# Attention into a max-out FFN: weight products ahead of batch 0, a log-and-exp softmax for batch 0, softmax steps issued singly

## The chip, the cores and the metric

The kernel runs on one core of a Trainium2 chip. The metric is the time of one execution on the device in microseconds (us), the median of several executions.

The engines have short names in the profile: PE multiplies matrices (PEld is its loading of weights), DVE works on vectors, ACT evaluates functions and copies, POOL and SP here mainly start transfers (DMAs). Each engine works through its own queue in order.

## The reference, cut to what matters

For each of 8 batches and 8 heads, a sequence of 576 positions is first summed into 32 memory slots, and then each position reads from those slots. The result, 4608 rows of 512, goes through an FFN with the maximum of three products as its activation.

```python
# q, k, v: (8, 8, 576, 64)   phi: (8, 8, 576, 32)   w1, w2, w3: (512, 768)   w_out: (768, 512)
a = np.exp(phi - max over positions);  a = a / (sum over positions)
k_m = einsum('bhsm,bhsd->bhmd', a, k)
v_m = einsum('bhsm,bhsd->bhmd', a, v)
scores = (q @ k_m.T) / 8
attn = softmax(scores over the 32 slots)
x = attn @ v_m                       # heads side by side: 4608 x 512
h = np.maximum(np.maximum(x @ w1, x @ w2), x @ w3)
out = h @ w_out
```

## The kernel before, in words

**Algebra.** Three rearrangements carry the kernel. First, max(x w1, x w2, x w3) is written as max(x (w1-w3), x (w2-w3), 0) + x w3. Hence `w_diff` subtracts w3 from w1 and w2 in place, a relu takes the place of one maximum, and the x w3 part goes straight to the output through w3 @ w_out, which is computed once (`w3_t` transposes w3, `w3_o` multiplies by w_out). Second, x is never formed: x w = attn (v_m w), so per batch `fold` multiplies the small v_m (32 slots per head) by w1-w3, w2-w3 (giving `wp`) and by w3 @ w_out (giving `wp3`). Third, phi has no maximum taken out before its exp; the normalisation is a division of the sums by the sum of exps, which a column of ones beside k and v delivers.

**Steps of one batch.** The letters are those of the order at the end of the kernel:

- L, H: load phi, k, v, q (0, 1, 2, 3); H loads half of batch 0's k or v. phi of batch 0 goes through SP's queue, every other load through POOL's, which also converts to bf16. Y: load w1, w2, w3 (0, 1, 2) or w_out (3), also on POOL.
- E: `att_exp`, exp of phi on ACT. B: `att_kv`, the sums over positions of k, v and ones on PE (72 small matmuls); part 0 is k and ones, part 1 is v alone. N: `att_kv_norm`, on DVE, divides the sums. K: `att_kv_t` transposes them on PE and copies the result out as `kvt`. Q: `att_q`, two 32x32-block transposes of q on DVE.
- S: `att_score`, scores on PE in two groups of heads (g = 0, 1), each with its exp on ACT to `e2`.
- X: `att_mul`, the softmax over slots for one group, five DVE instructions in a row: block transpose to `t` (line 313), sum (315), reciprocal (316), multiplication (317), transposing back into `attn` (323).
- D: `fold`, copied out by ACT or DVE. F: `ffn1`, 12 groups per batch, each of 4 matmuls of 288 columns (line 367); an even one ends in a relu (to `h1`), an odd one in a maximum with it on DVE (line 380, to `hT`). T: `ffn2`, a tile of 128 output rows, 8 matmuls of 512 columns (lines 398, 407), a copy and a store through SP. T4 is the tile that straddles two batches.
- W: `w3_t`. O: `w3_o`. V: `w_diff`. I: the identity. Z: n warm-up matmuls on a tile of zeros (line 128), whose result nobody reads.

**Buffers.** All PSUM tiles share one pool, `acc_pool`, of four tiles; a matmul group waits until an earlier tile has been read. `work` holds two of each tile. `evacuate` chooses between ACT and DVE by a table, and "!" behind a step swaps its choice:

```python
    EVAC = {"D": "avaaa", "T": "vavav", "K": "v", "W": "vvv", "O": "aaaa", "F": "aaaaaa"}
```

**Order.** The schedule is written out by hand: a string of steps such as `F8@0` (step F, number 8, batch 0), issued one after the other. This fixes each engine's queue; semaphores alone decide when a queued instruction starts. The first lines before:

```
        H3@0 H0@0 H2@0 I@0 H1@0 E@0 Z38@0 B@0 L3@0 N@0 Y2@0 Z3@0 K@0 Q0@0 Q1@0 Z7@0 S@0 X0@0
        Z6@0 W2@0! W0@0 Y3@0 Y0@0 W1@0 Z10@0 O1@0 O3@0 X1@0 V1@0 V0@0 O2@0 O0@0 D1@0 Y1@0 L0@1
```

So POOL loads v, k, q of batch 0, then w3, w_out, w1, w2, then batch 1; PE does batch 0's sums and scores first, then the w3 products, then the folds of batch 0 by the already subtracted weights.

Of the kernel before, what the change touches and what calls it, by code (L numbers as in the profile page):

```python
# [15 lines left out]
def kernel(  # L16
# [24 lines left out]
    FT = DF // P
    SH = S // 2
# [76 lines left out]
    warm = const.tile([P, BANK], BF16, name="warm")  # L119
    nc.vector.memset(warm, 0.0)  # L120
    nc.vector.memset(kvos[0][:, 2], 1.0)
    nc.vector.memset(kvos[1][:, 2], 1.0)

    def warm_up(n):
# [44 lines left out]

    w12 = w_sb[:, :, 0:2].rearrange("p j i f -> p j (i f)")  # L170

    FIRST = {0: (0, 512), 1: (512, 768), 2: (768, 1024), 4: (1024, 1536)}

    def columns(b, n):
        return FIRST[n] if b == 0 else (n * BANK, (n + 1) * BANK)

    def w_diff(n):

        c, end = FIRST[n]
        while c < end:  # L180
            e = min(end, (c // DF + 1) * DF)
            nc.vector.tensor_tensor(
                out=w12[:, :, c:e],
                in0=w12[:, :, c:e],
                in1=w_sb[:, :, 2, c % DF : c % DF + e - c],
                op=ALU.subtract,
            )
            c = e

    st = {}

# [56 lines left out]
    def att_kv_t(b, swap, part=None):  # L251

        s = st[b]
        ns = {None: slice(0, 3), 0: slice(1, 3), 1: slice(0, 1)}[part]
        ps = acc_pool.tile([P, 3, P], BF16, name="kvtp", tag="acc")
        for n in range(3)[ns]:
            nc.tensor.transpose(ps[:, n], s["kvn"][:, n], ident)
        if part != 1:
            s["kvt"] = work.tile([P, 3, P], BF16, name="kvt")
        evacuate("K", 0, swap, s["kvt"][:, ns], ps[:, ns])  # L260

    def att_q(b, n):

# [12 lines left out]
    def att_score(b):  # L276

        s = st[b]
        kvt, qT = s["kvt"], s["qT"]
        e2 = s["e2"] = work.tile([P, NG, S], BF16, name="e2")  # L280
        if b % 2 == 0:
            attns[b // 2] = work.tile([P, NG, 2 * S], BF16, name="attn")
        sc = [
            acc_pool.tile([P, 2, BANK], FP32, name="sc", tag="acc") for _ in range(NG)
        ]
        for h in range(2):
            for j in range(NP):
                for a in range(NG):
                    for t in range(2):
                        r = slice(R * (2 * a + t), R * (2 * a + t + 1))  # L290
                        nc.tensor.matmul(  # L291
                            sc[a][M * j : M * (j + 1), t, 0:SH],
                            lhsT=kvt[r, 1 + h, M * j : M * (j + 1)],
                            rhs=qT[r, j, :, :, h],
                            start=(h == 0),
                            stop=(h == 1),
                            tile_position=(R * (2 * a + t), M * j),
                        )
        for a in range(NG):
            nc.scalar.activation(  # L300
                out=e2[:, a].rearrange("p (t r c) -> p t r c", t=2, c=NC),
                in_=sc[a][:, :, 0:SH].rearrange("p t (c r) -> p t r c", c=NC),
                func=AF.Exp,
                scale=0.125,
            )

    def att_mul(b, g):
        s = st[b]
        e2 = s["e2"][:, g]
        t = work.tile([P, S // HP, R, 2], BF16, name="t", tag=f"t{g}")  # L310
        tf = t.rearrange("p n r e -> p (n r e)").bitcast(FP32)
        tv = t.rearrange("p n r e -> p n e r")
        nc.vector.transpose(out=tf, in_=e2.bitcast(FP32))  # L313
        sm = work.tile([P, S // HP, 2], FP32, name="sm", tag=f"sm{g}")
        nc.vector.tensor_reduce(out=sm, in_=tv, op=ALU.add, axis=mybir.AxisListType.X)  # L315
        nc.vector.reciprocal(out=sm, in_=sm)  # L316
        nc.vector.tensor_tensor(  # L317
            out=t,
            in0=t,
            in1=sm.unsqueeze(2).to_broadcast([P, S // HP, R, 2]),  # L320
            op=ALU.mult,
        )
        nc.vector.transpose(  # L323
            out=attns[b // 2][:, g, (b % 2) * S : (b % 2 + 1) * S].bitcast(FP32), in_=tf
        )

    wps, wp3s = {}, {}
# [1 line left out]
    def fold(b, n, swap):  # L329

        s = st[b]
        lo, hi = (0, DM) if n == 3 else columns(b, n)
        if n == 3:
            wp3s[b] = quad.tile([P, NG, DM], BF16, name="wp3")
        elif b not in wps:
            wps[b] = work.tile([P, NG, 2 * DF], BF16, name="wp")
        ps = acc_pool.tile([P, NG, BANK], FP32, name="wps", tag="acc")
        for j in range(NP):
            for a in range(NG):
                r = slice(HP * a, HP * (a + 1))  # L340
                nc.tensor.matmul(  # L341
                    ps[M * j : M * (j + 1), a, 0 : hi - lo],
                    lhsT=s["kvt"][r, 0, M * j : M * (j + 1)],
                    rhs=(w3o if n == 3 else w12)[r, j, lo:hi],
                    start=True,
                    stop=True,
                    tile_position=(HP * a, M * j),
                )
        evacuate(
            "D", n, swap, wp3s[b] if n == 3 else wps[b][:, :, lo:hi], ps[:, :, 0 : hi - lo]  # L350
        )
# [110 lines left out]
    def issue(b, n, swap):  # L462

        i = int(n[1:]) if len(n) > 1 else None
        {
            "I": lambda: make_identity(nc, ident),
            "Y": lambda: load_w(i) if i < 3 else load_wo(),
            "L": lambda: load_ph(b) if i == 0 else load_q(b) if i == 3 else load_kv(b, i - 1),
            "H": lambda: load_kv(b, i % 2, halves[i // 2]),
            "E": lambda: [att_exp(b, h) for h in (halves if b == 0 else [slice(0, NP)])],  # L470
            "B": lambda: att_kv(b, i),
            "N": lambda: att_kv_norm(b, i),
            "K": lambda: att_kv_t(b, swap, i),
            "Q": lambda: att_q(b, i),
            "S": lambda: att_score(b),
            "X": lambda: att_mul(b, i),
            "D": lambda: fold(b, i, swap),
            "F": lambda: ffn1(b, i, swap),
            "T": lambda: ffn2(b, i, swap),
            "W": lambda: w3_t(i, swap),  # L480
            "O": lambda: w3_o(i, swap),
            "V": lambda: w_diff(i),
            "Z": lambda: warm_up(i),
        }[n[0]]()


    for w in """
        H3@0 H0@0 H2@0 I@0 H1@0 E@0 Z38@0 B@0 L3@0 N@0 Y2@0 Z3@0 K@0 Q0@0 Q1@0 Z7@0 S@0 X0@0
        Z6@0 W2@0! W0@0 Y3@0 Y0@0 W1@0 Z10@0 O1@0 O3@0 X1@0 V1@0 V0@0 O2@0 O0@0 D1@0 Y1@0 L0@1
        D0@0! D3@0 V2@0 F10@0 V4@0 L1@1 F8@0 L3@1 F6@0 D2@0 F0@0! F2@0 D4@0 F3@0 F4@0 E@1 L2@1  # L490
        F1@0 F11@0 F7@0 L0@2 F9@0 F5@0 B0@1 T3@0 N0@1 L0@3 K0@1! Q0@1 T2@0! B1@1 Q1@1 S@1 E@2
        L2@2 L1@2 L0@4 N1@1 K1@1 T1@0 X0@1 D0@1 D1@1! L3@2 T0@0! D3@1 L1@3 L2@3 L3@3 D2@1 X1@1
        F6@1! F0@1 F1@1 F2@1 F4@1 F7@1 F5@1 E@3 F8@1 F3@1 F10@1 F11@1 F9@1 B@2 N@2 L0@5 Q0@2
        T1@1 L1@4 E@4 K@2 T4@1! Q1@2 S@2 T2@1! D0@2 D1@2! T0@1! X0@2 D3@2 B@3 X1@2 D2@2 T3@1
        N@3 F6@2 Q0@3 Q1@3 F0@2 F1@2 F8@2 F7@2 L2@4 F4@2 K@3 L3@4 L1@5 F10@2 F9@2 S@3 L2@5
        F11@2 F2@2 E@5 F5@2 F3@2 D2@3 D1@3! X0@3 X1@3 T2@2! D0@3 B@4 N@4 D3@3 T0@2! Q1@4 T3@2
        F4@3 F6@3 K@4 F8@3 Q0@4 F9@3 F2@3 F0@3 F7@3 F1@3 F10@3 L3@5 F11@3 D0@4 B@5 D1@4! D2@4
        T1@2 L0@6 L1@6 N@5 Q0@5 K@5 L2@6 F3@3 F5@3 S@4 E@6 Q1@5 T4@3! L0@7 X0@4 S@5 T1@3 D1@5!
        X1@4 D0@5 T2@3! X1@5 L3@7 D2@5 B@6 D3@4 F10@4 N@6 E@7 X0@5 T3@3 F8@4 F6@4 F9@4 F11@4
        F2@4 F4@5 L3@6 Q1@7 F7@4 F6@5 L1@7 F5@5 F8@5 Q1@6 F0@4 F7@5 F4@4 K@6 L2@7 Q0@7 F5@4  # L500
        Q0@6 T0@3! F3@4 F1@4 F0@5 F1@5 F2@5 F10@5 F3@5 D2@6 B@7 D3@5 D3@6 T3@4 N@7 K@7 F9@5
        F11@5 S@6 T4@5! S@7 T3@5 D1@6! D1@7! X0@6 D3@7 T0@5! X0@7 T2@4! D0@7 D0@6 D2@7 T1@4
        T1@5 X1@7 X1@6 F6@6 F8@6 F10@6 F2@7 F3@7 F0@6 F7@6 F9@6 F2@6 F3@6 F1@6 F4@7 F11@6 F10@7
        F4@6 F11@7 F6@7 F0@7 F5@7 F8@7 F9@7 F1@7 T0@4! F7@7 F5@6 T0@7! T1@7 T1@6 T0@6! T2@7!
        T2@5! T2@6! T3@6 T4@7! T3@7
    """.split():
        n, b = w.rstrip("!").split("@")
        issue(int(b), n, w.endswith("!"))
# [30 lines left out]
```

## Time and profile before

| what | value |
|---|---|
| median of 3 executions | 169.34 us (169.15 to 169.76) |
| the profiled execution | 170.24 us, of which a span of 168.5 us is in the trace |
| granted PE clock, mean | 0.996 |
| POOL's loads (q0) | 21.43 MB, 66.4% of the 16 DMA engines' span |
| SP's output stores and phi of batch 0 (q1) | 9.90 MB, 16.5% |
| FFN first layer, line 367 | 384 matmuls, 50.8 us busy |
| FFN second layer, lines 398 and 407 | 254 matmuls, 68.6 us busy |
| warm-up matmuls, line 128 | 62 records, 16.8 us busy |
| softmax on DVE, lines 313 to 323 | 16 of each of the five, mean 455, 753, 266, 758, 478 ns |
| copies of the folds, 1024 columns, ACT | 30, mean 1028 ns |

The span runs from the first to the last recorded instruction of one execution, so parts of it are compared with other spans, not with the median. A row of a group gives the engine's busy time in it; matmuls overlap one another, so the time for which PE is bound is less than their number times their mean.

### The profile page before, as it was taken

To read this page: it belongs to the slowest core of one execution; us is meant where nothing else is said; L and a number is where in the kernel's file an instruction comes from. 1 tells how busy PE (TensorE), PEld (TensorE's weight loads), DVE (VectorE), ACT (ScalarE), POOL (GpSimd) and SP (SyncE) were. 2 spreads that over 40 slices of the span, in tenths; PEclk is the share of its full clock that TensorE was granted. 3 is DMA by queue.
4 is the path that set the end of the run, shared out by engine and by line. 5 is a ranking of instruction groups with operands and counts; after the bars stand their busy time and mean duration, and the time that the engine had idled before them with its cause. 6 is when DMAs were issued, how large, how long until landed. Compare 5 with 4: busy or idle time off the path is not lost.

```text
span 168.5 us, 4603 instructions
## 1 busy us (share of the span) xinstructions
PE 157.6 (94%) x1971; PEld 86.9 (52%) x1992; DVE 110.3 (65%) x198; ACT 98.9 (59%) x145; POOL 28.4 (17%) x43
## 2 busy tenths in 40 slices
PE   7998799999879999999998999999999999999991
PEld 2443433674338535755574356666433578644450
DVE  5406876895587859879877999997599556610000
ACT  4200514943798279798666999638768876322420
POOL 7952100041171312403110500000000000000000
PEclk9999999999999999999999999999999999999998
DMA  5999999999999999999999999951113310033433
GB/s 154 147 204 212 206 209 244 244 208 342 262 287 259 208 228 327 247 234 208 234 296 244 288 251 260 235 101 64 68 62 128 121 66 6 0 125 143 168 125 126
DMA packets 21973, 31.76 MB, mean 189 GB/s; under 512 B 1216, under 2 KB 16576, under 8 KB 21952
## 3 DMA queue, kind: packets, MB, share of 16 engines
q0 software_dynamic: 16080, 21.43, 66.4%
q1 hardware_dynamic: 5728, 9.90, 16.5%
q8 instruction: 15, 0.25, 0.5%
q10 hardware_dynamic: 144, 0.13, 0.2%
q14 instruction: 6, 0.05, 0.1%
HBM read 39.32 MB, written 9.44 MB: 289 GB/s over the span
## 4 chain that ended last, share of the span: by engine, by line
PE 75%; DVE 19%; issue 2%; ACT 1%; ACTq 0%
PE acc L367 27%; PE po L398 20%; PE po L128 7%; PE po L407 6%; DVE sm L315 5%; DVE t L317 4%; PE wps L341 3%; PE kvp L212 3%; PE po L161 3%; DVE attn L323 3%; DVE t L313 2%; PE sc L291 2%; DVE sm L316 2%; ACT e L300 1%; PE po L416 1%
## 5 line engine op out<-in xcount | busy, mean ns | idle before, releaser
L367 PE MATMUL acc<-attn,wp 128*128 128x288 bf16 x384 | 50.8, 286 | 1.6 <-DVE attn L323 1.4
L398 PE MATMUL po<-wo_sb,hT 128*128 128x512 bf16 x192 | 50.2, 380 | 0.9
L367 PEld LDWEIGHTS <-wp 128*128 128x128 bf16 x384 | 36.5, 98 | 14.6 <-issue 2.0
L380 DVE TENSOR_TENSOR hT<-acc,h 128x576 bf16<-128x576 f32 x48 | 34.5, 752 | 13.0 <-PE acc L367 6.3
L141 ACT COPY ot<-po 128x512 f32<-128x512 f32 x35 | 20.7, 591 | 28.9 <-PE po L407 24.4
L139 ACT ACTIVATE h<-acc 128x576 bf16<-128x576 f32 x46 | 28.5, 655 | 8.6 <-PE acc L367 7.6
L398 PEld LDWEIGHTS <-hT 128*128 128x128 bf16 x210 | 19.1, 98 | 24.2 <-issue 4.6
L141 ACT CAST wp<-wps 128x1024 bf16<-128x1024 f32 (+1 forms) x31 | 29.7, 1014 | 0.9 <-PE wps L341 0.9
L300 ACT ACTIVATE e<-sc 128x576 bf16<-128x576 f32 x16 | 9.6, 653 | 16.5 <-PE sc L291 16.5
L407 PE MATMUL po<-wp,attn 128*128 128x512 bf16 x62 | 18.4, 379 | 0.0
L128 PE MATMUL po<-warm 128*128 128x512 bf16 x62 | 16.8, 430 | 1.4 <-DVE warm L120 1.2
L317 DVE TENSOR_TENSOR t<-t,sm 128x576 bf16<-128x576 bf16 x16 | 12.1, 758 | 0.5
L315 DVE TENSOR_REDUCE sm<-t 128x18 f32<-128x576 bf16 x16 | 12.1, 753 | 0.6
L269 DVE STREAM_TRANSPOSE qT<-qq 128x576 f32<-128x576 f32 x16 | 11.9, 761 | 0.0
L128 PEld LDWEIGHTS <-warm 128*128 128x128 bf16 x64 | 6.6, 108 | 9.9 <-issue 3.7
L90 POOL DMA_DIRECT2D ph<-in_phi_dram x7 | 5.3, 760 | 32.5 <-ACT e L199 27.8
L456 DVE COPY ot<-po 128x256 f32<-128x256 f32 x1 | 0.4, 425 | 15.8 <-PE po L447 15.8
L199 ACT ACTIVATE e<-ph 128x1152 bf16<-128x1152 f32 (+1 forms) x9 | 9.5, 1060 | 1.7 <-DMA ph<-in_phi_dram 1.7
L313 DVE STREAM_TRANSPOSE t<-e 128x288 f32<-128x288 f32 x16 | 7.3, 455 | 4.0 <-ACT e L300 4.0
L407 PEld LDWEIGHTS <-attn 128*128 128x128 bf16 x62 | 6.1, 98 | 7.3
L94 POOL DMA_DIRECT2D kvo<-in_k_dram x9 | 6.7, 744 | 15.5 <-PE wps L341 13.1
L102 POOL DMA_DIRECT2D qq<-in_q_dram x8 | 6.0, 750 | 16.4 <-DVE qT L269 15.7
(46 smaller groups left out, 110.7 us busy)
## 6 DMA issues: line engine op xcount, KB each, us to landing
out_dram<-ot SPq DMA_DIRECT2D x35, 256.0 KB, 2.3
qq<-in_q_dram POOLq DMA_DIRECT2D x8, 576.0 KB, 18.1
ph<-in_phi_dram POOLq DMA_DIRECT2D x7, 576.0 KB, 19.4
kvo<-in_k_dram POOLq DMA_DIRECT2D x7, 576.0 KB, 15.7
kvo<-in_v_dram POOLq DMA_DIRECT2D x7, 576.0 KB, 18.2
w_sb<-in_moe_w_dram POOLq DMA_DIRECT2D x3, 768.0 KB, 19.6
wo_sb<-in_moe_w_out_dram POOLq DMA_DIRECT2D x1, 768.0 KB, 16.7
ph<-in_phi_dram SPq DMA_DIRECT2D x2, 288.0 KB, 3.1
```

The lines of the kernel that those rows point to most:

```text
L128: nc.tensor.matmul(po[:, 0:BANK], lhsT=warm[:, 0:P], rhs=warm, start=True, stop=True)
L139: nc.scalar.activation(out=out_, in_=in_, func=AF.Relu)
L141: nc.scalar.copy(out=out_, in_=in_)
L269: nc.vector.transpose(out=s["qT"][:, j].rearrange("p j c r e -> p (j c r e)").bitcast(FP32), in_=loaded[b]["q"][:, j].rearrange("p j c d - ...
L300: nc.scalar.activation(out=e2[:, a].rearrange("p (t r c) -> p t r c", t=2, c=NC), in_=sc[a][:, :, 0:SH].rearrange("p t (c r) -> p t r c", ...
L313: nc.vector.transpose(out=tf, in_=e2.bitcast(FP32))
L315: nc.vector.tensor_reduce(out=sm, in_=tv, op=ALU.add, axis=mybir.AxisListType.X)
L317: nc.vector.tensor_tensor(out=t, in0=t, in1=sm.unsqueeze(2).to_broadcast([P, S // HP, R, 2]), op=ALU.mult,)
L367: nc.tensor.matmul(acc[:, h, 0:SH], lhsT=wps[b][:, g, w * DF + ft * P : w * DF + (ft + 1) * P], rhs=attn[:, g, c0 : c0 + SH], start=(g == ...
L380: nc.vector.tensor_tensor(out=hT[:, ft, (b % 2) * S : (b % 2 + 1) * S].rearrange("p (h n) -> p h n", h=2), in0=a, in1=s["h1", ft], op=ALU.max,
L398: nc.tensor.matmul(po, lhsT=hT[:, fc, c0 : c0 + P], rhs=wo_sb[:, fc, :], start=(n == 0), stop=False,)
L407: nc.tensor.matmul(po, lhsT=attn[:, g, c0 : c0 + P], rhs=wp3s[b][:, g, :], start=False, stop=(g == NG - 1),)
```

## The change

It does five things.

1. POOL's queue: w3 and w_out are loaded first, then k, q, v of batch 0, then w1, w2. The order has the w3 products (W, O) ahead of and between batch 0's first steps.
2. Batch 0's k (and ones) are summed ahead of v, as two parts, as batch 1 was before; its v sums follow the scores.
3. Batch 0's softmax is no longer done by DVE transposes. A matmul with a block-diagonal constant `blkones` (four 32x32 blocks of ones) gives every slot the sum over its head's slots (M), ACT takes Ln and then Exp with scale -1 of it (R), and one DVE multiplication makes attn (X).
4. The five softmax instructions of the other batches become steps of their own, a, s, c, m, X, placed singly in the order.
5. Batch 0's folds by w1 and w2 use the unsubtracted weights: a second set of matmuls with a negated copy of v_m (`kvtn`) and w3 is summed into the same PSUM tile. The columns of batch 0's folds are four times 384 instead of 512, 256, 256, 512. `w_diff` comes later, in pieces of 512 columns, for batches 1 to 7.

The whole order string is new, for all batches. The diff, cut to its core:

```diff
+    blkones = const.tile([P, P], BF16, name="blkones")
+    nc.vector.memset(blkones, 0.0)
+    for i in range(P // M):
+        nc.vector.memset(blkones[M * i : M * (i + 1), M * i : M * (i + 1)], 1.0)
...
-    FIRST = {0: (0, 512), 1: (512, 768), 2: (768, 1024), 4: (1024, 1536)}
+    FIRST = {0: (0, 384), 1: (384, 768), 2: (768, 1152), 4: (1152, 1536)}
...
     def w_diff(n):
-        c, end = FIRST[n]
+        c, end = n * BANK, (n + 1) * BANK
...
         evacuate("K", 0, swap, s["kvt"][:, ns], ps[:, ns])
+        if b == 0 and part != 0:
+            s["kvtn"] = const.tile([P, P], BF16, name="kvtn")
+            nc.scalar.mul(out=s["kvtn"], in_=ps[:, 0], mul=-1.0)
...
+    def ones_sum(b, g):
...
+        for h in range(2):
+            nc.tensor.matmul(
+                sm[:, h, 0:SH],
+                lhsT=blkones,
+                rhs=e2[:, g, h * SH : (h + 1) * SH],
+                start=True,
+                stop=True,
+            )
...
+    def ones_rec(b, g):
...
+        nc.scalar.activation(
+            out=ln.rearrange("p (h n) -> p h n", h=2),
+            in_=sm[:, :, 0:SH],
+            func=AF.Ln,
+        )
+        r = work.tile([P, S], FP32, name="r")
+        nc.scalar.activation(out=r, in_=ln, func=AF.Exp, scale=-1.0)
...
+    def ones_mul(b, g):
+        s = st[b]
+        nc.vector.tensor_tensor(
+            out=attns[b // 2][:, g, (b % 2) * S : (b % 2 + 1) * S],
+            in0=s["e2"][:, g, 0:S],
+            in1=s["r", g],
+            op=ALU.mult,
+        )
+
+    def att_t(b, g):
...
+    def att_sum(b, g):
...
+    def att_rec(b, g):
...
     def att_mul(b, g):
...
+    def att_back(b, g):
...
+        terms = [(s["kvt"][:, 0], w3o[:, :, lo:hi] if n == 3 else w12[:, :, lo:hi])]
+        if b == 0 and n != 3:
+            terms.append((s["kvtn"], w_sb[:, :, 2, lo % DF : lo % DF + hi - lo]))
+        for i, (lhs, rhs) in enumerate(terms):
             for j in range(NP):
                 for a in range(NG):
...
+                        start=(i == 0),
+                        stop=(i == len(terms) - 1),
...
+        Y2@0 I@0 Z29@0 W1@0 W0@0 Y3@0 W2@0 H2@0 H0@0 Z9@0 O3@0! E@0 L3@0 O0@0 B0@0 N0@0 O2@0
+        K0@0! Q0@0 H3@0 H1@0 O1@0 Q1@0 Y0@0 S@0 Z2@0 M0@0 R0@0 B1@0 Y1@0 N1@0 M1@0 R1@0 L0@1
+        K1@0 L1@1 D3@0 X0@0 Z5@0 D1@0! X1@0 D0@0 F10@0 F8@0 F0@0 F4@0 V0@0 F2@0! D2@0 D4@0 V1@0
+        F6@0 F1@0 F5@0 F11@0 F7@0 L3@1 F3@0 F9@0 E@1 B0@1 L2@1 N0@1 L0@2 Q0@1 T2@0! Q1@1 K0@1!
+        T1@0 S@1 V2@0 B1@1 L1@2 E@2 a0@1 s0@1 a1@1 N1@1 s1@1 T3@0 K1@1 c1@1 D0@1 D1@1! c0@1
+        m0@1 L2@2 D2@1 L3@2 m1@1 X0@1 T0@0! X1@1 F10@1 F4@1 L0@3 F11@1 F8@1 F0@1 F5@1 F2@1 F1@1
+        F9@1 F6@1 F7@1 F3@1 B@2 D3@1 T3@1 N@2 Q1@2 Q0@2 K@2 E@3 T4@1! L1@3 L2@3 S@2 a0@2 s0@2
+        c0@2 T2@1! L3@3 a1@2 m0@2 s1@2 D1@2! L0@4 c1@2 m1@2 X1@2 D3@2 T1@1 T0@1! X0@2 D0@2!
...
```

## Prediction

> **What bounds the kernel now.** I read the page's first two parts for the engine that sets the time, then the table by stage for where that engine has holes, then the timeline of the two places with holes, then what the holes wait for.
>
> Parts 1 and 2 of the page (busy time; tenths busy in 40 slices of 4.21 us):
>
> ```profile
> span 168.5 us, 4603 instructions
> PE 157.6 (94%) x1971; PEld 86.9 (52%) x1992; DVE 110.3 (65%) x198; ACT 98.9 (59%) x145; POOL 28.4 (17%) x43
> PE   7998799999879999999998999999999999999991
> ```
>
> PE is busy nearly throughout, but not all of it is work: the row of the warm-up matmuls (line 128) has 62 of them at the start. The table by stage puts the other visible hole between 40 and 50 us (busy 3.98 and 3.76 of 5 us, 2.26 us idle), while each 10 us stage from 50 to 160 us idles 0.05 to 0.49 us, 1.6 us in all. So two places can give time: everything before the first FFN matmul, and batch 1's softmax.
>
> The timeline of the start (start, length, engine, line, what):
>
> ```profile
> 12.12 0.94 PE L212 MATMUL kvp<-kvo,e 64*32 64x192 bf16 x72
> 14.80 1.43 DVE L269 STREAM_TRANSPOSE qT<-qq 128x576 f32<-128x576 f32 x2
> 19.14 1.51 PE L153 MATMUL pt<-ident,w_sb 128*128 128x128 bf16 x24 [1.21 <-DMA w_sb<-in_moe_w_dram]
> 23.03 5.34 PE L161 MATMUL po<-wo_sb,w3T 128*128 128x512 bf16 x23 [0.21 <-DVE sm L316]
> 26.74 1.83 DVE L182 TENSOR_TENSOR w_sb<-w_sb 128x1024 bf16<-128x1024 bf16 x2 [2.42 <-DMA w_sb<-in_moe_w_dram]
> 28.30 0.73 PE L341 MATMUL wps<-w_sb,kvt 64*32 64x256 bf16 x16
> 29.42 1.79 PE L367 MATMUL acc<-attn,wp 128*128 128x288 bf16 x12
> ```
>
> Every stage starts where a transfer lands: k and v at 12.1, q before 14.8, w3 at 19.1, w1 at 26.7. Behind w1 come w_diff (1.83), the last w3@w_out product (PE until 28.37), the folds and their copies; the first FFN matmul starts at 29.42.
>
> Timeline around batch 1 (in brackets the idle time before and what ended it):
>
> ```profile
> 40.80 0.75 PE L212 MATMUL kvp<-kvo,e 64*32 64x64 bf16 x72
> 43.28 1.19 ACT L300 ACTIVATE e<-sc 128x576 bf16<-128x576 f32 x2 [1.78 <-PE sc L291]
> 43.96 0.48 DVE L313 STREAM_TRANSPOSE t<-e 128x288 f32<-128x288 f32 x1 [0.32 <-ACT e L300]
> 49.11 0.48 DVE L323 STREAM_TRANSPOSE attn<-t 128x288 f32<-128x288 f32 x1
> 49.64 5.79 PE L367 MATMUL acc<-attn,wp 128*128 128x288 bf16 x46 [1.24 <-DVE attn L323]
> ```
>
> Batch 1's scores end only at 43.3 (0.96 us of it an unexplained wait in mid-score), DVE then runs both groups' softmax in one piece to 49.6, and PE runs out of other work. After 49.64 PE has no hole of size.
>
> **What the Trainium skill says.** "VectorE: DVE Perf Modes", section "The perf-mode tier table", has tensor_reduce and any fp32 tensor_tensor at one element per cycle; the rows here agree (0.753 and 0.758 us for 576). "ScalarE: Activation LUTs", "Table sets: the hidden batching unit", says that natural_log_exp_and_others holds both exp and ln; line 62 preloads it, the trace has one table load (1.28 us at 0.74), so I cost the new Ln no reload. "DMA: Bandwidth & Descriptors", "Issuing engines are not separate DMA queues", says that all queues share 16 DMA engines; the trace agrees in that POOL issues the four weights by 8.5 us and they land one after another until 30.4.
>
> **The transfers.** Issue plus time to landing gives w3 5.49+13.6=19.1, w_out 6.22+16.7=22.9, w1 7.04+19.6=26.7, w2 7.8+22.6=30.4: 768 KB each 3.8 us, so 576 KB take 2.85. The change only permutes what POOL's queue has ahead of w1 (SP's queue keeps phi of batch 0 alone until the first output; POOL's identity, 0.5, now stands between w3 and w_out, while w3 is still flowing), so w1 still lands at 26.7, w2 at 30.4, then as before phi, k, q and v of batch 1 at 31.9, 34.7, 37.5 and 40.4. Within the permuted part I read the old landings as a function of bytes landed (phi included: k and v complete at 1728 KB, q 2304, w3 3072, w_out 3840): w3 about 10, w_out 13.4, k 16.7, q 20.1, v 22.9.
>
> **Part by part, batch 0.** w3's 24 transposes (1.5) run at 10, the w_out products (5.3) from 13.4, split around k's sums. That removes them from in front of w1 (hidden earlier: PE has only warm-ups there; 64 fall to 45, worth nothing). The phi exps are early on ACT, whose time is free. k: 0.7 PE, 0.76 DVE, transposes, all done by 19 while q is awaited. q: two transposes 1.45, so 21.55; scores 0.45; exp 0.65 each (row of line 300): 22.65 and 23.25. New softmax: two 288-column matmuls per group on PE (0.3, beside ACT), Ln and Exp on ACT. Both take 0.65 (nearest row, 653 ns; bounds 0.6 to 0.75): 23.9, 24.55, 25.2, 25.85. Each multiply is 0.76 on DVE, the last ending 26.65. It takes ten DVE steps off (2 x 2.74 = 5.5) and puts back 1.5; ACT gets 2.6. The constant's five small memsets run before 7 us, when DVE has nothing else. v: sums from 22.9, its transpose by 24.3, the minus copy behind the second Exp on ACT (0.25): 26.1; the w_out fold's copy 1.03: 27.1.
>
> Then w1 (26.7): fold D1 with 16 matmuls rather than 8, 0.5 with drain, to 27.25. The four folds of batch 0 are 384 columns wide each and get 32 matmuls more, 0.16 per fold when eight run side by side (two folds of 512 take 0.43 in the chain), bounds 0 to 0.3; they replace the subtraction in front of the folds (0.69 and 1.22 before the first two). D1's copy of 768 columns on ACT is 0.82 (between the rows 0.617 for 512 and 1.028 for 1024): 28.05. **First FFN matmul 28.05 rather than 29.42: 1.35 gained**; the three w_diffs (1.22, 1.38, 1.22) move behind the folds, where only batch 1 needs them.
>
> PE then needs 0.49 per group (the chain of waits has 8 matmuls of line 367 in 0.98) and 1.72 per T (1.29+0.43 there). ACT is full: D0's copy 28.9, four relus to 31.5, D2 and D4 (w2 at 30.4 is in time) 32.35 and 33.2, one relu 33.85. F1 waits for D2, so PE loses 0.6 here, and its 12 groups end about 35.3 rather than 36.47. DVE has the second w_diff until 32.85 and six maxima of 0.75 to 37.5, then norm 0.76, two q transposes to 39.8.
>
> **Batch 1.** On PE: k's sums to 36.0, T2 (waits for the last maximum, 38.1), k's transposes, T1 to 40.2, scores by 40.65, v's sums (40.4 landed) to 41.35. Exps end 41.3 and 41.95. On DVE the last w_diff ends 41.05; then the separated steps with v's norm and copy wedged between: 0.48+0.75+0.48+0.29+0.75+0.23+0.27+0.27+0.76+0.76+0.48+0.48 = 6.0, so 41.3 to 47.4. PE meanwhile has T3, K1, three folds, T0 and still idles about 2 us. FFN of batch 1 starts 47.5 rather than 49.64: 2.15; D3 of 0.2 is left for later: **1.95 gained, carried on**. It is not added to the 1.35; it contains it.
>
> Later batches: the same matmuls; steps of softmax in other places. Batch 2's chain as I place it (scores 58.2, ten steps 5.5, end 64.5) ends before PE has finished its fillers (65.4), so nothing is waited for. v2 and k2 are no longer queued on POOL behind phi of batch 3, which waited for an exp until 36.08; B of batch 3 needs them near 64.6, my landing is 61. I set the rest to zero, with bounds: all of the 1.6 idle gained, or 4.8 lost (case c).
>
> Sum against its own span: 168.5-1.95 = 166.55. Applied to the median of the shown runs (169.34): 167.4.
>
> **Rivals.** (a) *The gain is eaten at batch 1.* If ACT's pile-up or a late q delays DVE's maxima by 1.5 us, F of batch 1 starts near 49.1: 168.9. For: DVE's q transposes end only 0.25 earlier than before by my own placing. Against: scores no longer split by 0.96, and come 2.6 us earlier in exp.
> (b) *More than placed.* The separate steps also close what is left: half of batch 1's 2 idle and of the later 1.6: 1.8 more, 165.6. For: three F starts in the trace wait on DVE's attn or its steps. Against: little idle is there to close, and it is spread thin.
> (c) *Slower: DVE softmax chains become the wait of PE.* In batch 1 the wedged-in norm and copies stretch exp-to-attn from 5.65 to 6.1. If in batches 2 to 7 chains end 0.8 after PE's fillers, 6 x 0.8 = 4.8 less 1.95: 172.2; it decides from 0.33 per batch, where the gain is gone. For: DVE is on the chain that ended last for 19%, PE has no filler to spare around 92 to 105. Against: DVE is relieved of 5.5-1.5 in batch 0, and the T groups (1.72 each) lie behind the scores.
> (d) *It doesn't do what it says:* early w3 and w_out hide nothing if q's landing at 20.1 is later, since F start moves with it one for one beyond 0.15: q at 21.6 gives back the 1.35, and with it 1.3 of the 1.95: about 168.7, together with (a).
>
> **How the numbers follow.** A measurement here can tell about 0.5%, 0.85 us. The forecast has 0.52 (own range 166.4 to 168.4), (b) 0.16, (a) and (d) 0.14, (c) 0.18. Faster: forecast, (b) and a little of (a): 0.69; same 0.13; slower 0.18. The range goes from 165.4, below (b), to 170.6, into (c).
>
> **What would show it.** Right: first line 367 matmul near 28.05, with w1 landing at 26.7; ACT back to back with exp, Ln, copies and relus from 22 to 34; line 367 of batch 1 at 47.5 behind DVE attn; idle of PE after 50 us still 1 to 2 us. Wrong step by step: q landing after 20.3 (start), a second table load (1.28), exps of batch 1 after 42 (case a), PE idle above 0.3 per 10 us at DVE attn in the later stages (case c). The whole is wrong if the span is above 168.5.

## The result and the profile after

The changed kernel takes 166.98 us (median of 4 runs, 166.54 to 167.58) beside 169.55 for the kernel before on the same chip: a ratio of 0.985, interval 0.981 to 0.989. Measured again later on another chip it took 167.37 us (6 runs), ratio 0.987, interval 0.985 to 0.990. The forecast was 167.4. So the size is right. Whether it is right for the reasons given is another question. The prediction spoke of three places: the start, batch 1 and the later batches. Only batch 1 came out as forecast; a loss at the start and a gain in the later batches, neither of them in its sum, nearly cancelled.

The page of the changed kernel, its first two parts and the engines' shares of the chain that ended last:

```profile
span 165.8 us, 4795 instructions
PE 154.6 (93%) x2063; PEld 86.1 (52%) x2081; DVE 105.0 (63%) x196; ACT 100.6 (61%) x150; POOL 28.3 (17%) x43
PE   7968987999899999999999999999999999999990
...
PE 73%; DMA 20%; ACT 2%; issue 1%; POOL 1%; POOLq 0%; ACTq 0%
```

The same line of the kernel before, from part 4 of its page:

```profile
PE 75%; DVE 19%; issue 2%; ACT 1%; ACTq 0%
```

The span fell by 2.7 us. In the row of tenths, the 8 and 7 that stood at 42 to 50 us have become a single 8; the start, up to 29 us, has more digits below 9 than before. DVE, 19% of the chain before, is no longer on it; transfers (20%) stand in its place.

The timeline of the start in the changed kernel:

```profile
11.49 1.51 PE L157 MATMUL pt<-ident,w_sb 128*128 128x128 bf16 x24 [1.49 <-DMA w_sb<-in_moe_w_dram]
15.49 2.75 PE L165 MATMUL po<-wo_sb,w3T 128*128 128x512 bf16 x12 [0.55 <-DMA wo_sb<-in_moe_w_out_dram]
...
27.69 0.36 PE L403 MATMUL wps<-w_sb,kvt 64*32 64x384 bf16 x8
28.28 1.50 ACT L145 CAST wp<-wps 128x768 bf16<-128x768 f32 x2 [0.38 <-PE wps L403]
29.13 1.03 PE L429 MATMUL acc<-attn,wp 128*128 128x288 bf16 x7 [0.60 <-ACT wp L145]
```

w3 and w_out do arrive early and are multiplied while batch 0 loads. From w1's landing (27.64) to the first FFN matmul it takes 1.5 us, where the kernel before needed 2.8 (26.64 to 29.42). But w1 landed 1.0 later than before. The first FFN matmul, 29.13, is only 0.29 earlier than before.

The timeline around batch 1:

```profile
40.70 0.48 PE L295 MATMUL sc<-qT,kvt 32*32 32x288 bf16 x32
41.29 1.20 ACT L304 ACTIVATE e<-sc 128x576 bf16<-128x576 f32 x2
41.98 0.48 DVE L350 STREAM_TRANSPOSE t<-e 128x288 f32<-128x288 f32 x1 [0.73 <-ACT e L304]
42.50 0.75 DVE L358 TENSOR_REDUCE sm<-t 128x18 f32<-128x576 bf16 x1
43.17 0.47 DVE L350 STREAM_TRANSPOSE t<-e 128x288 f32<-128x288 f32 x1
43.56 0.25 DVE L233 TENSOR_TENSOR kvn<-kvp,rden 128x128 bf16<-128x128 f32 x1
...
46.27 0.83 DVE L380 STREAM_TRANSPOSE attn<-t 128x288 f32<-128x288 f32 x2
47.79 2.38 PE L429 MATMUL acc<-attn,wp 128*128 128x288 bf16 x18
```

The scores run in one piece and 2 us earlier than the second piece of before (42.76), the two groups' steps alternate with the norm of v between them, and the FFN of batch 1 starts at 47.79. Before, two of its matmuls ran at 47.99 and the rest waited for the second group's attn until 49.64. There is no bracket at 47.79: PE came to it straight from other work, not from a wait for attn.

PE between 50 and 160 us (length, busy, and so on by engine; then clock, DMA share, GB/s), first before, then after:

```profile
50.00:160.00 110.00, 108.39 (x1393) 62.70 (x1407) 78.22 (x145) 75.69 (x112) 11.19 (x15) 1.00 0.75 177
```

```profile
50.00:160.00 110.00, 109.17 (x1405) 62.49 (x1415) 77.39 (x146) 75.02 (x111) 11.19 (x15) 1.00 0.76 185
```

The 1.61 us of idle have become 0.83. Most of that is one stage: between 90 and 110 us PE was busy 19.28 before and 19.89 after.

One execution per kernel is traced. That of before took 170.24, 0.7 above the median. How far single moments vary can be read from a later run, old_until_batch1_done, which has before's order up to this point: its first FFN matmul is at 28.74 and the rest of batch 1's FFN goes on at 48.61, 0.7 and 1.0 earlier than in the trace of before. So differences of single moments of up to 1 us are left to the timed comparisons that follow.

### The profile page after: what moved, and what is told of

It reads as the page before. It is cut to its first block, busy times and chain, and to the rows that moved or that the text cites. A ratio compares the mean times of both kernels' runs of the same rounds, so it can differ in the third digit from the quotient of the medians.

```text
span 165.8 us, 4795 instructions
## 1 busy us (share of the span) xinstructions
PE 154.6 (93%) x2063; PEld 86.1 (52%) x2081; DVE 105.0 (63%) x196; ACT 100.6 (61%) x150; POOL 28.3 (17%) x43
## 4 chain that ended last, share of the span: by engine, by line
PE 73%; DMA 20%; ACT 2%; issue 1%; POOL 1%; POOLq 0%; ACTq 0%
PE po L460 26%; PE acc L429 25%; DMA ph<-in_phi_dram 13%; DMA wo_sb<-in_moe_w_out_dram 8%; PE po L469 7%; PE wps L403 4%; PE kvp L213 3%; PE po L165 3%; PE sc L295 2%; PE po L478 1%; PE po L501 1%; ACT e L200 1%; PE kvtp L258 1%; POOL w_sb L108 1%; ACT w3o L145 0%
## 5 line engine op out<-in xcount | busy, mean ns | idle before, releaser
L429 PE MATMUL acc<-attn,wp 128*128 128x288 bf16 x384 | 50.1, 286 | 0.7 <-ACT wp L145 0.6
L145 ACT COPY ot<-po 128x512 f32<-128x512 f32 x34 | 20.0, 588 | 26.7 <-PE po L469 18.4
L132 PE MATMUL po<-warm 128*128 128x512 bf16 x43 | 12.7, 446 | 1.3 <-DVE warm L120 1.2
L273 DVE STREAM_TRANSPOSE qT<-qq 128x576 f32<-128x576 f32 x16 | 11.7, 753 | 1.1 <-DMA qq<-in_q_dram 1.1
L145 ACT CAST w3o<-po 128x512 bf16<-128x512 f32 x3 | 1.8, 586 | 15.5 <-PE po L165 15.5
L94 POOL DMA_DIRECT2D kvo<-in_v_dram x9 | 6.6, 742 | 25.7 <-PE wps L403 15.8
L350 DVE STREAM_TRANSPOSE t<-e 128x288 f32<-128x288 f32 x14 | 6.4, 463 | 6.9 <-ACT e L304 6.8
L358 DVE TENSOR_REDUCE sm<-t 128x18 f32<-128x576 bf16 x14 | 10.3, 739 | 0.3
L372 DVE TENSOR_TENSOR t<-t,sm 128x576 bf16<-128x576 bf16 x14 | 10.3, 744 | 0.2
L213 PE MATMUL kvp<-kvo,e 64*32 64x192 bf16 (+2 forms) x720 | 8.7, 229 | 0.6 <-DMA kvo<-in_v_dram 0.5
L213 PEld LDWEIGHTS <-e 64*32 64x32 bf16 x720 | 7.5, 90 | 3.2 <-issue 1.7
```

Source lines behind the costliest of these rows:

```text
L132: nc.tensor.matmul(po[:, 0:BANK], lhsT=warm[:, 0:P], rhs=warm, start=True, stop=True)
L145: nc.scalar.copy(out=out_, in_=in_)
L213: nc.tensor.matmul(kvp[M * j : M * (j + 1), a, 0:nd], lhsT=s["e"][r, j, c, :], rhs=kv[r, cols, j, c, :], start=(c == 0), stop=(c == NC - 1 ...
L273: nc.vector.transpose(out=s["qT"][:, j].rearrange("p j c r e -> p (j c r e)").bitcast(FP32), in_=loaded[b]["q"][:, j].rearrange("p j c d - ...
L358: nc.vector.tensor_reduce(out=sm, in_=s["t", g].rearrange("p n r e -> p n e r"), op=ALU.add, axis=mybir.AxisListType.X,)
L372: nc.vector.tensor_tensor(out=t, in0=t, in1=s["sm", g].unsqueeze(2).to_broadcast([P, S // HP, R, 2]), op=ALU.mult,)
```

## The experiments

The theory at this point: the gain comes from the order after batch 0 (batch 1's single steps and what follows), and the new start gives nothing, since w1 came later. The rival is the prediction's own: the early start is carried on to batch 1. The first two runs exchange the halves.

### The start of before with the new order after it (old_head_new_rest)

Batch 0 as before: loads, DVE softmax, subtraction ahead of the folds and the old column split; from `B0@1` on the order of the change.

```diff
-        Y2@0 I@0 Z29@0 W1@0 W0@0 Y3@0 W2@0 H2@0 H0@0 Z9@0 O3@0! E@0 L3@0 O0@0 B0@0 N0@0 O2@0
+        H3@0 H0@0 H2@0 I@0 H1@0 E@0 Z38@0 B@0 L3@0 N@0 Y2@0 Z3@0 K@0 Q0@0 Q1@0 Z7@0 S@0 X0@0
...
-        F6@0 F1@0 F5@0 F11@0 F7@0 L3@1 F3@0 F9@0 E@1 B0@1 L2@1 N0@1 L0@2 Q0@1 T2@0! Q1@1 K0@1!
+        F1@0 F11@0 F7@0 L0@2 F9@0 F5@0 B0@1 N0@1 Q0@1 T2@0! Q1@1 K0@1! T1@0 S@1 B1@1 L1@2 E@2
```

> The old order up to the last first-layer group of batch 0 (old loads, batch 0's softmax in five DVE steps, w1 and w2 subtracted before the folds), then the new order from batch 1's sums on, softmax steps placed singly. Theory A, from the two traces (the first FFN matmul came only 0.29 us earlier, batch 1's came 1.85 earlier): the gain is made by the order of batch 1 and later. Then the first FFN matmul is at 29.4, that of batch 1 near 48, and the median lies 2 to 2.4 us below the kernel before (ratio 0.986 to 0.988). Theory B, as the prediction had it: the gain begins in the new start. Then batch 1 starts near 49.5 and the ratio is 0.996 to 1.000.

Measured: 166.11 us (165.38 to 167.03), ratio 0.979, interval 0.976 to 0.982. That is a larger gain than theory A had forecast (0.986 to 0.988). From its timeline:

```profile
29.10 1.79 PE L429 MATMUL acc<-attn,wp 128*128 128x288 bf16 x12
...
40.48 0.47 PE L295 MATMUL sc<-qT,kvt 32*32 32x288 bf16 x32
...
46.33 0.83 DVE L380 STREAM_TRANSPOSE attn<-t 128x288 f32<-128x288 f32 x2
...
47.22 2.98 PE L429 MATMUL acc<-attn,wp 128*128 128x288 bf16 x23
```

With the old start the first FFN matmul comes at the same time (29.10 against 29.13), and batch 1 is no later (47.22 against 47.79). The start that was to be worth 1.35 us isn't needed for the gain. This version beats both kernels; against the change's 0.985 and 0.987 it is 0.6 to 0.8% better, and its interval does not overlap the second of the two. (A nearly equal version, scores_before_t1 below, took 0.983, so the advantage may be smaller.)

### The new start with the old order after it (new_head_old_rest)

The change's order to `F9@0 E@1`, then the order of before, with the five softmax steps in a row again (line 542 of the kernel, the X step).

```diff
-            "X": lambda: (ones_mul if b == 0 else att_back)(b, i),
+            "X": lambda: ones_mul(b, i) if b == 0 else (att_t(b, i), att_sum(b, i), att_rec(b, i), att_mul(b, i), att_back(b, i)),
...
-        F6@0 F1@0 F5@0 F11@0 F7@0 L3@1 F3@0 F9@0 E@1 B0@1 L2@1 N0@1 L0@2 Q0@1 T2@0! Q1@1 K0@1!
+        F6@0 F1@0 F5@0 F11@0 F7@0 L3@1 F3@0 F9@0 E@1 B0@1 L2@1 T3@0 N0@1 L0@2 L0@3 K0@1! Q0@1
```

> The new order up to the last first-layer group of batch 0, then the old order from batch 1's sums on, each softmax in five DVE instructions in a row; the third subtraction stands behind batch 1's scores, where DVE had a hole. Theory A: the start alone brings 0.3 us, ratio 0.996 to 1.000, FFN of batch 1 near 49.3. Theory B: ratio 0.985 to 0.989, FFN of batch 1 near 48.

Measured: 170.44 us (169.40 to 172.05), ratio 1.005, interval 1.003 to 1.007. Its timeline at batch 1:

```profile
49.40 0.48 DVE L380 STREAM_TRANSPOSE attn<-t 128x288 f32<-128x288 f32 x1
49.93 5.30 PE L429 MATMUL acc<-attn,wp 128*128 128x288 bf16 x42 [1.19 <-DVE attn L380]
```

Although its first FFN matmul is at 28.93, batch 1 again waits 1.19 us for attn and starts at 49.93, like before. The new start alone costs 0.5%, some 0.8 us, where I had expected a gain of up to 0.4%. The rival falls.

### The order of before until batch 1's first layer is done (old_until_batch1_done)

This separates batch 1 from the batches behind it: before's order up to `F9@1`, the change's from `B@2` on (batch 0 and batch 1 with five steps in a row).

```diff
-        F9@1 F6@1 F7@1 F3@1 B@2 D3@1 T3@1 N@2 Q1@2 Q0@2 K@2 E@3 T4@1! L1@3 L2@3 S@2 a0@2 s0@2
+        E@3 F8@1 F3@1 F10@1 F11@1 F9@1 B@2 T3@1 N@2 Q1@2 Q0@2 K@2 T4@1! S@2 a0@2 s0@2
```

> The old order to the end of batch 1's first FFN layer, the new order from batch 2's sums on. If the gain lies in batch 1 (FFN of batch 1 at 47.2 against 49.6 in the run with the old head and the new rest), most of it is lost: FFN of batch 1 near 49.5 and ratio 0.992 to 0.996, the rest being the 0.8 us of PE idle that the later stages lost in the changed kernel. If it lies in the later batches: 0.980 to 0.985.

Measured: 167.45 us (167.35 to 168.07), ratio 0.989, interval 0.986 to 0.991. Batch 1 has its old shape (scores in two pieces, 1.24 us waited for attn, FFN at 48.61), and still the kernel is 1.9 us faster than before. So batches 2 to 7 give 1.9 us by themselves (1.5 to 2.4 by the interval); the ratio lies between my two expectations, so the gain has two places. PE's idle time between 50 and 160 us is 0.69 (before 1.61), which is 0.9 of it; the other 1.0 I can't assign to a row: the matmuls are the same, and TensorE's tiling switches from `B@2` on are as many (34 and 34). The step from this run to the one with the old start (0.989 to 0.979, disjoint intervals) is batch 1's own order: 1.6 us, or 0.9 if scores_before_t1 (0.983) is taken in its place.

### Single places or groups (five_in_a_row, five_at_the_last)

Does the new order need the softmax steps one by one, or would the order alone do? In the change's order, each group of batches 1 to 7 gets its five steps together, once where its first step `a` stands, once where the last, `X`, stands.

```diff
-        T1@0 S@1 V2@0 B1@1 L1@2 E@2 a0@1 s0@1 a1@1 N1@1 s1@1 T3@0 K1@1 c1@1 D0@1 D1@1! c0@1
+        T1@0 S@1 V2@0 B1@1 L1@2 E@2 a0@1 s0@1 c0@1 m0@1 X0@1 a1@1 s1@1 c1@1 m1@1 X1@1 N1@1 T3@0
```

> The changed kernel with the softmax of batches 1 to 7 issued as five instructions in a row for each group, at the place where the changed order has its first (step a). If placing the steps singly is what makes the new order of the later batches good: v's norm and copy and then the folds of batch 1 wait for the whole row on DVE, FFN of batch 1 comes 0.5 to 1 later, and the same in some later batches: 1 to 2.5 us slower than the changed kernel, ratio to before 0.991 to 1.000. Rival: only the order of the large steps counts and single placing is worth nothing: 0.983 to 0.987.

Measured: 177.75 us (176.81 to 180.18), ratio 1.048, interval 1.045 to 1.052. This missed both of my expectations by far. The trace is of the slowest of its six executions, 180.18. Its timeline at batch 1, and two rows of its table by stage (the third number from the end is the clock):

```profile
48.12 0.48 DVE L380 STREAM_TRANSPOSE attn<-t 128x288 f32<-128x288 f32 x1
48.53 0.25 DVE L233 TENSOR_TENSOR kvn<-kvp,rden 128x128 bf16<-128x128 f32 x1
48.84 0.29 PE L258 MATMUL kvtp<-ident,kvn 128*128 128x128 bf16 x1 [3.83 <-DVE kvn L233]
...
40.00:50.00 10.00, 5.55 (x137) 2.50 (x143) 7.79 (x15) 4.26 (x7) 2.23 (x3) 0.93 1.17 246
50.00:60.00 10.00, 10.00 (x75) 5.62 (x58) 2.50 (x4) 6.55 (x10) 0.00 (x0) 0.73 1.17 254
```

The norm of v, 0.25 us long, stands behind ten softmax steps in DVE's queue; PE's transpose waits 3.83 us for it, and the folds and the FFN of batch 1 (54.24) behind that. PE is busy only 5.55 of the 10 us from 40 to 50. The wait is followed by a halved clock (0.51 from 48.5 to 55.5), so part of the 10 us is clock and not queue. The mean clock of all six executions is 0.978 to 0.988; from that I estimate 2 to 4 us. In later batches PE waits another 3.9 us for maxima and an output copy on DVE (2.4 and 1.5).

For the second of the two runs:

```diff
-        m0@1 L2@2 D2@1 L3@2 m1@1 X0@1 T0@0! X1@1 F10@1 F4@1 L0@3 F11@1 F8@1 F0@1 F5@1 F2@1 F1@1
+        D2@1 L3@2 a0@1 s0@1 c0@1 m0@1 X0@1 T0@0! a1@1 s1@1 c1@1 m1@1 X1@1 F10@1 F4@1 L0@3 F11@1
```

> The changed kernel with the softmax of batches 1 to 7 as five instructions in a row again, now at the place where the changed order has its last step (X), so that nothing else on DVE waits behind them. If what cost 10 us in the run five_in_a_row was the norm and the copies queued behind the row: most of that is gone, but each attn comes later by the steps that could have run before: 1 to 3 us slower than the changed kernel, ratio to before 0.990 to 1.005. If single placing is itself worth little: 0.983 to 0.988.

Measured: 177.39 us (175.81 to 179.59), ratio 1.043, interval 1.040 to 1.047. This missed what I expected (0.990 to 1.005) by far. The first row of its table of PE's waits (us in total, times, longest), then the same row of before:

```profile
PE acc L429 <- DVE attn L380: 7.7, 6, 2.3
...
PE acc L367 <- DVE attn L323: 1.4, 2, 1.2
```

Now nothing is blocked in front, but attn comes late: six FFN starts wait 7.7 us, where before had two with 1.4. The clock stayed high here (mean 0.999 in the traced execution). So the new order needs the single steps: with ten steps in one piece, either the norm and the copy wait behind them or attn comes too late for the other work that PE has. Whether the old order would gain from single steps too was not tried.

### Batch 0's softmax back on DVE (batch0_softmax_on_dve, dve_softmax_clean)

The Ln-and-Exp softmax of batch 0 is undone, first by putting the DVE steps where M and R stood.

```diff
-        K0@0! Q0@0 H3@0 H1@0 O1@0 Q1@0 Y0@0 S@0 Z2@0 M0@0 R0@0 B1@0 Y1@0 N1@0 M1@0 R1@0 L0@1
+        K0@0! Q0@0 H3@0 H1@0 O1@0 Q1@0 Y0@0 S@0 Z2@0 a0@0 s0@0 c0@0 m0@0 B1@0 Y1@0 N1@0 a1@0
+        s1@0 c1@0 m1@0 L0@1 K1@0 L1@1 D3@0 X0@0 Z5@0 D1@0! X1@0 D0@0 F10@0 F8@0 F0@0 F4@0
```

> The changed kernel with one part undone: batch 0's softmax again by the five DVE instructions, at the places of the sums and of Ln and Exp. If the log-and-exp form is worth what its place says: DVE's attn of batch 0 ends near 29.8, first FFN matmul near 30 rather than 29.13, and since DVE is full from 34 to 40 the loss stays: 0.5 to 0.9 us slower than the changed kernel, ratio to before 0.988 to 0.990. If the wait for w1 and w2 hides it: ratio 0.985, as the changed kernel.

Measured: 170.88 us (170.10 to 171.24), ratio 1.007, interval 1.005 to 1.009. That looks like 4 us for the softmax, but it isn't. Its table by stage (us, length, busy of PE, PEld, DVE, ACT, POOL, then clock):

```profile
24.00:26.00 2.00, 0.57 (x72) 0.45 (x47) 1.90 (x5) 0.14 (x1) 0.74 (x1) 1.00 1.16 209
26.00:28.00 2.00, 0.23 (x1) 0.10 (x1) 1.90 (x5) 0.00 (x0) 0.00 (x0) 1.00 1.17 216
28.00:30.00 2.00, 1.17 (x9) 0.41 (x11) 1.33 (x4) 0.93 (x2) 0.74 (x1) 0.60 1.09 323
30.00:32.00 2.00, 1.97 (x27) 0.65 (x34) 0.00 (x0) 0.36 (x1) 0.14 (x1) 0.55 1.18 236
```

The copy of v's transpose (0.22 us, DVE) got queued behind the second group's steps until 28.37. PE, which needs it for the folds, was nearly idle from 24.6 to 28.6, and then had a clock of 0.60 and 0.55 in the next two stages of 2 us. The first FFN matmul came at 33.06. This run measured a queue and a clock, so I repeated it with the copy ahead of the second group and warm-ups in the gaps.

```diff
-        Z2@0 M0@0 R0@0 B1@0 Y1@0 N1@0 M1@0 R1@0 L0@1 K1@0 L1@1 D3@0 X0@0 Z5@0 D1@0! X1@0 D0@0
+        Z2@0 a0@0 s0@0 c0@0 m0@0 B1@0 Y1@0 N1@0 Z6@0 K1@0 D3@0 a1@0 s1@0 L0@1 c1@0 m1@0 L1@1
+        X0@0 X1@0 Z4@0 D1@0! D0@0 Z6@0
```

> Batch 0's softmax on DVE again, as in the run batch0_softmax_on_dve, but v's copy ahead of the second group's steps and warm-up matmuls in PE's gaps, so that the clock stays at 1.00 and the folds by w3 at w_out don't queue behind DVE. The bare price of ten DVE instructions against Ln and Exp: attn of batch 0 at 30.0, first FFN matmul 30.1 rather than 29.13, 0.7 to 1.2 slower than the changed kernel, ratio to before 0.989 to 0.993. If the earlier run's 4 us were the price of the instructions themselves and not of the gap: 1.005.

Measured: 167.41 us (167.10 to 167.63), ratio 0.988, interval 0.985 to 0.990, not to be told from the change's 0.985 and 0.987. The clock stayed at 1.00, the first FFN matmul came at 29.87, batch 1 at 47.89. In this trace the first FFN matmul follows w1's landing (27.23) by 2.6 us and not 1.5, so the start did get later, but at batch 1 almost nothing of that is left. By the medians the ACT softmax is worth 0 to 0.4 us, which is within the noise.

### The subtraction back in front of batch 0's folds (subtract_before_folds, subtract_clean)

The negated copy and its 32 matmuls are taken out; w1 and w2 are reduced by w3 before batch 0's folds, in pieces of 384 columns.

```diff
-        if b == 0 and n != 3:
+        if False:
...
-        K1@0 L1@1 D3@0 X0@0 Z5@0 D1@0! X1@0 D0@0 F10@0 F8@0 F0@0 F4@0 V0@0 F2@0! D2@0 D4@0 V1@0
+        K1@0 L1@1 D3@0 X0@0 Z5@0 V1@0 D1@0! X1@0 V0@0 D0@0 F10@0 F8@0 F0@0 F4@0 F2@0! V2@0 D2@0
```

> The changed kernel with another part undone: w3 is subtracted from w1 and w2 (four pieces of 384 columns) ahead of batch 0's folds, which have one set of matmuls; no negated copy. If the sum in PSUM is worth what it takes off the path behind w1: one piece 0.93 us, first FFN matmul near 29.9 to 30.1, 0.5 to 0.9 slower than the changed kernel at the end, ratio 0.988 to 0.990. Rival: w2, which lands at 31.6, is the gate of batch 0's first layer, and only its own piece of 0.93 counts once: 0.3 to 0.9 at the end of the layer; or nothing is left of it at batch 1, whose chain begins with DVE's six maxima: 0.985.

Measured: 171.86 us (170.75 to 173.02), ratio 1.013, interval 1.008 to 1.017. Again this measured a queue and a clock. The first FFN matmul came at 30.06, as expected. But PE's folds had four waits for subtractions, 4.8 us in all. The longest, 1.7 us, was for the third one, which stood behind the relu of F2 on DVE (32.73), and `X1@0` stood between the first two. The clock fell to 0.50 from 36 to 38 us. Once more with X1 in front of the subtractions, the third one in front of F2, and warm-ups in the gaps:

```diff
+        K1@0 L1@1 D3@0 X0@0 X1@0 Z9@0 V1@0 D1@0! V0@0 Z2@0 D0@0 F10@0 F8@0 F0@0 F4@0 V2@0
+        F2@0! D2@0 V4@0 D4@0 F6@0 F1@0 F5@0 F11@0 F7@0 L3@1 F3@0 F9@0 E@1 B0@1 L2@1 N0@1 L0@2
```

> The subtraction ahead of batch 0's folds again, as in the run subtract_before_folds, but batch 0's second attn multiplication ahead of the first subtraction on DVE, two subtractions around F2 and not in a row, and warm-up matmuls in PE's gap. The bare price of the subtraction: first FFN matmul 29.9 rather than 29.13, batch 0's first layer 1 to 1.8 later, 0.7 to 1.8 slower than the changed kernel, ratio to before 0.989 to 0.996. If the order on DVE was not the cause of that run's loss: 1.010 and more.

Measured: 168.27 us (166.92 to 170.26), ratio 0.991, interval 0.988 to 0.995. That is 0.4 to 0.6% above the change, with overlapping intervals. Its trace is of the fastest of the six executions (166.92), in which w1 landed early, at 26.14. From there to the first FFN matmul (28.54) it took 2.4 us, 0.9 more than with the change; batch 1 started at 47.69. So the folds without a subtraction save 0.9 us behind w1, and at the end between nothing and 1 us.

### k ahead of w3 in the loads (k_ahead_of_w3)

Only the loads change places: batch 0's two k pieces go in front of w3.

```diff
-        Y2@0 I@0 Z29@0 W1@0 W0@0 Y3@0 W2@0 H2@0 H0@0 Z9@0 O3@0! E@0 L3@0 O0@0 B0@0 N0@0 O2@0
+        H2@0 H0@0 Y2@0 I@0 Z29@0 W1@0 W0@0 Y3@0 W2@0 Z9@0 O3@0! E@0 L3@0 O0@0 B0@0 N0@0 O2@0
```

> The changed kernel with only the two loads of batch 0's k moved ahead of w3 and w_out in POOL's queue; nothing else is placed anew. In the three kernels with w3 first w1 landed at 27.2 to 27.7, in the kernels with the old head at 26.1 to 26.7. If large first transfers cost that 1 us: w1 at 26.7. If it is the sum of bytes and the ring on POOL that set it: 27.4 to 27.7 again. The time: W and O stand first on PE and get their weights 2.9 later, so 0 to 1.5 us slower than the changed kernel, ratio 0.985 to 0.994.

Measured: 167.89 us (167.46 to 168.22), ratio 0.991, interval 0.989 to 0.993. The issues of w3, w1 and w2 on POOL (number, shortest, median and longest ns, first and last start) and their times to landing, first in this run, then in the changed kernel:

```profile
L108 POOL DMA_DIRECT2D w_sb<-in_moe_w_dram x3: 777/795/802, 2.8 to 7.8; - x3
...
DMA to landing us min/median/max: 9.7/18.9/23.0
```

```profile
L108 POOL DMA_DIRECT2D w_sb<-in_moe_w_dram x3: 747/782/877, 1.2 to 11.7; - x3
...
DMA to landing us min/median/max: 10.2/19.8/20.6
```

w1, issued at 7.05 here and at 7.03 with the change, lands after 18.9 us (at 26.0) instead of 20.6 (at 27.64); w2 is issued at 7.8 instead of 11.7, where POOL had waited for w3's landing, and lands at 30.8 instead of 31.5. The bytes ahead of w1 are the same. That points to the order of the loads, but the landing also varies from run to run, so one trace is thin evidence.

All traces of this study together: with the loads in before's order (four) w1 lands at 26.0 to 26.6; in the change's order (nine) at 26.1 to 27.8, the middle one at 27.4. (My expectation had only three of these in view.) Within the nine, w1 is by and large the later, the later w3, the first of all, has landed: w3 at 9.06, 10.56 and 11.44 goes with w1 at 26.14 (subtract_clean), 26.72 (five_at_the_last) and 27.64 (the change). So with large pieces in front, most of what varies is settled in the first 11 us. The number of bytes moved doesn't decide it alone: the trace of before and the second trace of the change both average 189 GB/s over their first 26 us, and w1 lands at 26.64 and 27.78. At the 208 GB/s that both show from 12 us on, these 1.1 us are an estimated 0.24 MB of other loads that moved ahead of w1's last bytes.

The kernel here isn't faster for it, because scores now end at 24.2 rather than 23.0 and the first FFN matmul waits for batch 0's own chain (30.05). PE, idle for 2.3 us until w3 landed at 12.5, also had a clock of 0.50 from 14 to 16 us; the mean clock was 0.99 in all four executions.

### The best version's scores still earlier (scores_before_t1)

In the version with the old start, S of batch 1 is put in front of T1.

```diff
-T1@0 S@1
+S@1 T1@0
```

> The old head and new rest, with batch 1's scores issued ahead of the output tile T1 and not behind it. In that run the q transposes of batch 1 end at 39.7 and the scores come at 40.5, behind T1's 1.7 us; the DVE chain behind them sets the FFN of batch 1. If that chain is the bound: scores at 39.8, FFN of batch 1 0.6 earlier, ratio to before 0.974 to 0.977 against 0.979. If PE's own work is the bound there: T1 only moves its 1.1 us gap to another place, ratio 0.978 to 0.982.

Measured: 166.40 us (166.25 to 166.93), ratio 0.983, interval 0.981 to 0.985. Scores start 1.1 us earlier (39.35), the FFN of batch 1 only 0.1 (47.12): v's sums end at 42.4 rather than 42.5, the folds behind them start at 44.61 rather than 44.71, and the second group's steps behind the copy of v keep their place. No gain beyond the version it starts from; the ratio is 0.4% above it, with overlapping intervals, and the traced spans are alike (164.6 and 164.7).

The run with the change itself as a control:

> The changed kernel once more beside these, for a narrower interval: ratio 0.983 to 0.988.

Measured: 167.37 us (166.41 to 167.86), as told above. w1 landed at 27.8, the first FFN matmul came at 29.27, batch 1 at 47.30.

## Why the prediction was right in size and where it was wrong

**Transfers: wrong.** "So w1 still lands at 26.7, w2 at 30.4" failed: 27.64 and 31.5, and w1 at 27.8 in the second trace of the change. The pieces ahead of w1 were late too: w3 11.4 (forecast 10), w_out 15.4 (13.4), k 18.2 (16.7), q 21.0 (20.1), v 23.9 (22.9). I had taken landing times as a function of bytes landed. That function was read from one trace of an order that began with pieces of 288 KB; with two pieces of 768 KB in front w1 comes about 1 us later in the middle of nine traces, and varies over 1.6 us, where the old order varies over 0.7 in four. What makes the first large piece, w3, land anywhere between 9.06 and 11.44 isn't settled. The four weights that the prediction saw land one after another all went through POOL's queue, so they don't show how several queues share the engines.

**First FFN matmul: wrong, and with it the account of the gain.** "28.05 rather than 29.42: 1.35 gained" is the step that failed; measured 0.29 between the two traces. With all traces that share the start, nothing can be told: 28.74 to 29.42 in four with the old start, 28.21 to 29.27 in five with the new. The work behind w1's landing was priced well: it takes 1.5 us in each of the five and 2.8 in each of the four (1.35 forecast). The later landing ate the difference. Case (d) named this kind of loss, but by q, which landed at about 21 instead of 20.1, not by w1; attn of batch 0 was ready at 27.63, 1.5 us before it was used. Ln and Exp took 0.63 to 0.68 us where I had 0.65, and no second table load appears in the trace. Batch 0's layer ended at 36.2 rather than 35.3.

**Batch 1: right, by a different sum.** FFN forecast 47.5, measured 47.79 and 47.30. I had the 1.95 *contain* the 1.35 of the start. The old start with the new order gives 47.22, so the gain is that of batch 1's order alone. Part of the difference to 49.64 lies in the trace of before itself, since the same order gave 48.61 in another execution. The pause of 0.96 us in mid-score, whose going I counted on, is of this kind: with the old order it was 0.60 in the other trace, and in old_head_new_rest one of 0.76 stood in v's sums instead. Two terms were off and cancelled. The exps of batch 1 ended at 42.5, past the 42 that I had named as the sign of case (a), and the first transpose of the softmax began at 41.98 where I had 41.3. From there the twelve DVE instructions took 5.1 us (41.98 to 47.10) where I summed their durations to 6.0; before, the ten steps alone took 5.6 (43.96 to 49.59). And PE was idle 1.35 us from 40 to 50 where I left 2.

**Later batches: wrong size.** "I set the rest to zero, with bounds: all of the 1.6 idle gained, or 4.8 lost." The order from batch 2 on gives 1.9 us (1.5 to 2.4), about the upper bound or above it. Zero was the wrong middle: I had counted only idle time, and half of this gain is not idle time. Case (b), that the separate steps also close what is left, is what happened here; case (c) did not: in the changed kernel no FFN start of batches 2 to 7 stands in the waits for attn. Grouping shows how near (c) was: with the same order and the steps together, it is 8 us slower than before.

**The sum as it is.** By the timed comparisons: order of batches 2 to 7, 1.9 us gained; order of batch 1, 1.6 gained; new start, 1.0 to 1.4 lost (0.985 and 0.987 against 0.979). These add up to the measured 2.1 to 2.5 because the last is taken from the change itself. Measured on its own, with the old rest, the new start loses 0.8, and the sum would be 2.7. I had 1.95, from the middle one alone. That the total came out is luck: I missed a gain and a loss of nearly one size. Where the new start loses can't be put in one place, since its first FFN matmul is no later: in the trace PE waits 0.47 for an output copy in front of batch 1, and loses another 0.5 later. Nor was each of its parts undone: of the loads only k was moved.

## What to carry to other kernels

Where a queue works in order, price a change of order by what stands behind each wait, not by busy times: placing each group's five short DVE steps in one piece or singly made 10 us of 167, and a copy of 0.22 us behind five other steps, with the halved clock that followed, made 3.5. Test the parts of a large change by exchanging halves: this one was a gain of about 3.5 and a loss of about 1, and half of it was at least as good as the whole. Landing times read from one order of loads, and from one trace, don't hold for another order with larger pieces in front.

## What was not expected of the hardware

**Independent DVE steps overlap, dependent ones don't.** Before, each step of a group starts 0.03 to 0.04 us after the one it depends on has ended (43.96 + 0.48, next at 44.48); so do all 64 such pairs of that trace. In the changed kernel the second group's transpose starts at 43.17, 0.08 before the first group's sum ends (42.50 + 0.75). Over batch 2's ten steps this is 5.64 us before (61.36 to 67.00) and 5.16 after (60.02 to 65.18). The Trainium skill, "VectorE: DVE Perf Modes", section "The DRAIN you can't avoid", says that the next operation doesn't start until the pipe is empty, and that one which isn't held starts earlier. The traces agree in that both kinds of start occur; that being held is here the same as depending on the step before is my reading, and no run tests it. Alternating two chains saved about 0.5 us of DVE time in batch 2. Whether that shortened the kernel is not shown.

**Idle gaps of PE halve its clock.** "TensorE: Matmul & The Clock Gate", section "What's actually happening", gives half the full clock after at least one idle window of about 3.4 us. The runs show the half: 0.51 from 48.5 to 55.5 after a wait of 3.83 us in five_in_a_row, and 0.60 and 0.55 from 28 to 32 with the DVE steps in M's place, after gaps of 1.68 and 2.17 us with one short matmul between them. They don't give a length below which a gap is safe: in the second trace of the change one gap of 2.23 us (until 11.45) was followed by a clock of 0.50 from 11.5 to 14.5, while in five_at_the_last one of 2.25 us (until 49.59) left it at 1.00, as did the 1.2 us wait of before at batch 1. So a wait of PE can be paid twice, once as idle time and once in the clock.
